# Two MLPs behind an attention: where the raw words of the up weights land, and when two pairs of weights are decoded

## The chip, the cores and the metric

The kernel runs on one core of a Trainium2 chip. The metric is the device time of one execution in microseconds; the kernel before took 832.86, 834.61 and 835.45 us in three runs, median 834.61. Its engines are TensorE (PE: matrix products), VectorE (DVE) and ScalarE (ACT: elementwise work), GpSimd (POOL) and SyncE (SP, which issues DMAs). The engines work from queues of their own and wait for each other by semaphores.

## The reference

An attention over 4 batches of 544 rows in 8 heads of 64 (32 global rows that see everything, 512 local rows that see a band and the global ones), and behind it two MLPs of 2304 rows:

```
x = attention(q, k, v)                     # 2304 x 512
h = x @ w_in ;  g = where(h > 0, h, exp(min(h, 0)) - 1) ;  x = g @ w_out
h = x @ w_in2;  g = 0 below -1, h above 1, (h + 1)**2 / 4 between;  out = g @ w_out2
```

w_in is 512 x 2048, w_out 2048 x 512. The weights come as 64-bit numbers.

## The kernel before

The attention takes the first 127 us or so; then come the MLPs. PE works in a 32-bit format with a shortened mantissa, so every operand is split into a high and a low part and every product is three (low x high, high x low, high x high). The 64-bit weights are split on the chip by `decode` (L200): the two halves of each number are unpacked by seven steps on DVE (L217 to L240) and two on ACT (L214 and the copy of the high part, L238). Step L239, `power`, isolates the exponent and writes it over the raw words, which are no longer needed then; L240 makes the low part of it.

The hidden width of 2048 goes in blocks of 128 (`f`), mostly in pairs of blocks: pairs n = 0 to 5 belong to layer 0, 6 to 13 to layer 1. The four token batches of 512 go in two duos. For a pair and a duo, a 2 x 2 block product is made by seven products instead of eight (`quad`, four parts; each product is 6 matmuls, L1064). For it the weights of a pair are wanted as they are and in four mixtures (S1 to S4), and the tokens in seven forms (X11 to T4). `decode_in(n)` makes the weights: `words` (L868) loads the raw words, two DMAs of 512 KB into one of the two buffers `wraw` that all raw words and sums share; then `decode`, `whole` (high + low), four additions `mixed`, and their split (ACT L912, DVE L862). The result is `wi`, one tile per pair with the weights in its first half and the mixtures in the second, in one of three places (n mod 3). `decode_out(n)` does the same for the down weights (`wo`).

DVE also joins the products (`u`, L862), makes the nonlinearity (with ACT; `g`, `gl`), and adds down products to sums. Each product needs one of four PSUM banks in rotation, so PE's next product in a bank waits for DVE (or ACT, L1094) to have read the last one.

Between the layers the tokens' forms are made anew: `later_forms(duo)` takes the sums of layer 0 (`so_far`, loaded again from DRAM by L1163 and L1166), mixes them on DVE, splits each form (`split`: ACT L954, DVE L862) and stores it to DRAM (`keep`, L961). The forms of batches 2 and 3, `later_forms(1)`, come in the second half of chunk 2, those of batches 0 and 1 in chunk 3.

What sets the order: the program runs through 7 chunks of 17 events, one chunk per two pairs and some 87 us each. In an event one part of a `quad` is issued; `job_at` puts jobs (decodes, forms) on a line at an event of a chunk, and a job does a step per event. From the program so written a scheduler makes each engine's fixed order. All DMAs from SP go out in one order.

```
job_at(at + 1, decode_out(2 * c + 1))
job_at(at + 5, decode_in(2 * c + 2));  job_at(at + 8, decode_out(2 * c + 2))
c == 2: job_at(at + 9, later_forms(1), False)     else: job_at(at + 12, decode_in(2 * c + 3))
c == 3: job_at(at, decode_in(7)); job_at(at + 2, decode_out(7)); job_at(at + 4, later_forms(0), False)
```

Of the kernel before, what the change touches and what calls it, by code (L numbers as in the profile page):

```python
# [9 lines left out]
F32 = mybir.dt.float32  # L10
# [68 lines left out]
def band_attention_then_two_mlps(  # L79
# [120 lines left out]
    def decode(wtmp_p, raw, hi, lo):  # L200

        n = raw.shape[1]
        words = raw.bitcast(U32).rearrange("p (n two) -> p n two", two=2)
        low, high = words[:, :, 0], words[:, :, 1]
        top = wtmp_p.tile([P, n], U32, tag="top", name="top")
        if eng is pinned:
            power = wtmp_p.tile([P, n], U32, tag="power", name="power")
        else:
            power = raw.bitcast(U32)[:, 0:n]
        rest = wtmp_p.tile([P, n], U32, tag="rest", name="rest")  # L210
# [646 lines left out]

    pairs_in, slot = {}, {}

# [24 lines left out]
    def of_pair(n):  # L884

        layer, q = (0, n + 2) if n < 6 else (1, n - 6)
        return layer, (2 * q, 2 * q + 1)

    def decode_in(n):

        layer, fs = of_pair(n)
        raw = words(KT * P, [(w1, w2)[layer][f][:, 0:KT * P] for f in fs])
        yield
# [3 lines left out]
        for _ in decode(wtmp_p, raw, w[:, 0, 0:4 * BLOCK], w[:, 1, 0:4 * BLOCK]):  # L897
            pass
        yield
# [3 lines left out]
        whole = add(  # L903
            x, w[:, 0, 0:4 * BLOCK].bitcast(F32), w[:, 1, 0:4 * BLOCK].bitcast(F32)
        )
# [5 lines left out]
        hi = w[:, 0, 4 * BLOCK:]  # L911
        eng.scalar.activation(hi, y, AF.Copy)  # L912
        add(w[:, 1, 4 * BLOCK:], y, hi.bitcast(F32), ALU.subtract)
        pairs_in[n] = w
        rows_in[1, n] = lambda k, part: w[:, part, 0:4 * BLOCK].rearrange("p (f c) -> p f c", f=2)[
            :, :, k * P:(k + 1) * P
        ]
# [48 lines left out]
    def first_forms(duo):  # L966
# [20 lines left out]
        for i, pair in enumerate((((T2, x22), (T3, x12)), ((T1, x11), (T4, x21)))):  # L987
            if duo == 0:

                t = w_ps[0].tile([P, 2, 2, 2 * SL], F32R, tag=f"wi{i}", name="form")  # L990
            for k, (form, src) in enumerate(pair):
                out = new_form(form) if duo else [t[:, k, part] for part in range(2)]
# [7 lines left out]
    def later_forms(duo):  # L1000

# [43 lines left out]
    born = {(0, f, j): -LAG for f, j in [(f, j) for j in range(B) for f in EARLY][:UP_EARLY]}  # L1045
    made_forms, holds, summed, w_out_uses = set(), {}, {}, {}

# [10 lines left out]
    def product(n, duo, col, i, then):  # L1058

        need(lambda: n in pairs_in and holds.get(i) == (of_pair(n)[0], duo))  # L1060
        ps, w, x = up_bank(), pairs_in[n], slot[i]
        for k in range(2):
            for t, (a, b) in enumerate(((1, 0), (0, 1), (0, 0))):
                eng.tensor.matmul(  # L1064
                    ps,
                    w[:, a, col + k * P:col + (k + 1) * P],
                    x[b][:, k * SL:(k + 1) * SL],
# [77 lines left out]
    def pop():  # L1145
# [7 lines left out]
        else:  # L1153
# [3 lines left out]
            if f == fs[2 % len(fs)] and NF - 1 in fs:  # L1157

                if layer == 0 and j < 2:
                    if j == 0:  # L1160
                        spare.append(w_ps[1].tile([P, 2, 2 * BLOCK * 4], F32, tag="wi2", name="sums"))
                    so_far[layer, j] = spare[0][:, j % 2].rearrange("p (k n) -> p k n", k=KT)
                    eng.sync.dma_start(so_far[layer, j], sums[layer + 1, j])  # L1163
# [9 lines left out]

    spare = []
    pair_of = {(of_pair(n)[0], f): n for n in range(14) for f in of_pair(n)[1]}
# [81 lines left out]
    for c in range(7):  # L1257
        at = base + 17 * c
        if c == 3:

            job_at(at, decode_in(7))
            job_at(at + 2, decode_out(7))
            job_at(at + 4, later_forms(0), False)
# [4 lines left out]
        job_at(at + 1, decode_out(2 * c + 1))  # L1268
        if c < 6:
            job_at(at + 5, decode_in(2 * c + 2))  # L1270
            job_at(at + 8, decode_out(2 * c + 2))
            if c == 2:
                job_at(at + 9, later_forms(1), False)
            else:
                job_at(at + 12, decode_in(2 * c + 3))
    for g, (c, duo) in enumerate(groups):
# [90 lines left out]
```

## Time and profile before

| | before |
|---|---|
| median of 3 runs, us | 834.61 (832.86 to 835.45) |
| profiled execution, us | 831.0 |
| span of its trace, us | 829.2 |
| PE busy | 805.8 us, 97% |
| DVE busy | 683.4 us, 82% |
| ACT busy | 547.2 us, 66% |
| granted PE clock | 1.00 |
| DMA | 172.49 MB, mean 208 GB/s |

Start with the busy shares in equal windows of 20 us: a share over the whole span hides where an engine is full and where it isn't. Then look, in the window where PE is not full, at what ended each of its idle times (the timeline of PE), and go on to the engine named there. Times count from the span's start.

### The profile page before, as it was taken

The numbers are of one execution on the slowest core, as the hardware profiler recorded it, in microseconds if no ns is written. First come the engines' busy times: TensorE is split into PE (matmuls) and PEld (weight loads), VectorE is DVE, ScalarE is ACT, GpSimd is POOL, SyncE is SP. The second block draws the span as 40 slices with busy tenths as digits, with TensorE's granted clock in tenths as the row PEclk, the third lists the DMA queues.
The fourth block names the chain that finished last, engine by engine and source line by source line (L and its number), as shares of the span: only waits on it lengthen the run. The fifth ranks groups of instructions, "written<-read, shape, count | busy, mean of one in ns | idle before, by whom it ended". The sixth has DMA issues, their size and how long they took to land.

```text
span 829.2 us, 15816 instructions
## 1 busy us (share of the span) xinstructions
PE 805.8 (97%) x6058; PEld 659.1 (79%) x6058; DVE 683.4 (82%) x1276; ACT 547.2 (66%) x929; POOL 87.7 (11%) x146
## 2 busy tenths in 40 slices
PE   7899899999999999999999979999999999999998
PEld 5677778888888888888888856888888888888886
DVE  5898979997989789867879899999988797845563
ACT  5888865675576656656555658778867786766451
POOL 2232200000011111111000000000110202011000
PEclk9999999999999999999999999999999999999999
DMA  8988828787966498629727667539671995369533
GB/s 284 330 272 273 253 89 295 263 343 256 357 169 143 99 278 265 120 22 292 245 90 290 228 247 261 153 122 303 202 161 25 263 296 107 46 172 291 198 106 110
DMA packets 63676, 172.49 MB, mean 208 GB/s; under 512 B 8944, under 2 KB 9200, under 8 KB 62448
## 3 DMA queue, kind: packets, MB, share of 16 engines
q1 hardware_dynamic: 54096, 154.43, 53.7%
q0 software_dynamic: 9216, 16.78, 13.1%
q8 instruction: 48, 0.79, 0.4%
q10 hardware_dynamic: 288, 0.26, 0.1%
q14 instruction: 28, 0.23, 0.1%
HBM read 112.46 MB, written 58.98 MB: 207 GB/s over the span
## 4 chain that ended last, share of the span: by engine, by line
PE 82%; DVE 6%; DMA 5%; ACT 4%; issue 2%; SPq 0%; DVEq 0%; ACTq 0%
PE dn L369 38%; PE up L1064 29%; PE up L282 4%; PE up L294 2%; DMA wraw<-in_w 2%; PE dn L382 2%; DMA v_sb<-in_vwin 2%; ACT sn L147 1%; PE s L147 1%; PE up L147 1%; DVE u L862 1%; PE pt L147 1%; DVE xl L862 1%; ACT pT L147 1%; PE po L147 1%
## 5 line engine op out<-in xcount | busy, mean ns | idle before, releaser
L1064 PE MATMUL up<-xh,wi 128*128 128x512 f32 x784 | 259.9, 391 | 5.0 <-DVE u L862 2.5
L369 PE MATMUL dn<-gh,wo 128*128 128x512 f32 x608 | 181.4, 390 | 0.0
L1064 PEld LDWEIGHTS up<-xh,wi 128*128 128x128 f32 x784 | 147.2, 188 | 37.2 <-DVE u L862 3.6
L862 DVE TENSOR_TENSOR u<-up,u 128x512 f32<-128x512 f32 x196 | 131.8, 688 | 48.7 <-PE up L1064 47.6
L1064 PE MATMUL up<-xl,wi 128*128 128x512 f32 x392 | 152.8, 390 | 0.0
L369 PEld LDWEIGHTS dn<-gh,wo 128*128 128x128 f32 x608 | 114.0, 188 | 23.6
L353 POOL DMA_DIRECT2D sum<-ev x64 | 58.6, 1211 | 589.7 <-ACT ev L348 588.8
L331 ACT ACTIVATE gh<-g 128x512 fp32r<-128x512 f32 x123 | 77.0, 628 | 56.5 <-DVE g L314 27.8
L369 PE MATMUL dn<-gl,wo 128*128 128x512 f32 x304 | 111.8, 390 | 0.5 <-DVE gl L335 0.5
L335 DVE TENSOR_TENSOR gl<-g,gh 128x512 fp32r<-128x512 f32 x123 | 84.4, 689 | 17.3 <-ACT gh L331 17.2
L1064 PEld LDWEIGHTS up<-xl,wi 128*128 128x128 f32 x392 | 73.7, 188 | 14.7
L307 ACT ACTIVATE g<-u,half_sb 128x512 f32<-128x512 f32 x64 | 46.1, 721 | 42.8 <-DVE u L862 37.7
L369 PEld LDWEIGHTS dn<-gl,wo 128*128 128x128 f32 x304 | 57.0, 188 | 12.7 <-DVE gl L335 1.0
L369 PE MATMUL dn<-gh,xl 128*128 128x512 f32 x160 | 62.7, 393 | 0.5 <-DVE sum L356 0.4
L348 ACT ACTIVATE ev<-dn 128x512 f32<-128x512 f32 x96 | 53.5, 598 | 14.6 <-PE dn L369 13.5
L369 PE MATMUL dn<-gh,xh 128*128 128x512 f32 x160 | 62.4, 390 | 0.0
L316 DVE TENSOR_TENSOR g<-u,g 128x512 f32<-128x512 f32 x64 | 43.9, 688 | 20.9 <-ACT g L309 20.8
L369 PE MATMUL dn<-gl,xh 128*128 128x512 f32 x160 | 59.0, 390 | 0.0
L302 ACT ACTIVATE g<-u 128x512 f32<-128x512 f32 x48 | 30.2, 630 | 35.8 <-DVE u L862 29.4
L308 ACT ACTIVATE g<-g,one_sb 128x512 f32<-128x512 f32 x68 | 49.1, 721 | 1.4
L304 ACT ACTIVATE g<-g,one_sb 128x512 f32<-128x512 f32 x63 | 45.5, 722 | 1.5
L309 ACT ACTIVATE g<-g 128x512 f32<-128x512 f32 x68 | 42.8, 629 | 1.2
(190 smaller groups left out, 1354.1 us busy)
## 6 DMA issues: line engine op xcount, KB each, us to landing
wraw<-in_w SPq DMA_DIRECT2D x56, 512.0 KB, 6.6
xl<-form SPq DMA_DIRECT2D x42, 512.0 KB, 6.9
xh<-form SPq DMA_DIRECT2D x42, 512.0 KB, 8.7
v_sb<-in_vwin SPq DMA_DIRECT2D x64, 260.0 KB, 4.7
sum<-ev POOLq DMA_DIRECT2D x64, 256.0 KB, 8.0
form<-xh SPq DMA_DIRECT2D x24, 512.0 KB, 3.6
form<-xl SPq DMA_DIRECT2D x24, 512.0 KB, 4.7
sum<-ev SPq DMA_DIRECT2D x32, 256.0 KB, 4.7
```

The costliest lines, as they stand in the source:

```text
L147: return lambda *args, **kw: tc.keep_in_program_order(fn(*args, **kw))
L304: eng.scalar.activation(self.g, self.g, AF.Relu, bias=one_sb, scale=-1.0)
L307: eng.scalar.activation(self.g, self.ps, AF.Relu, bias=half_sb, scale=-0.5)
L308: eng.scalar.activation(self.g, self.g, AF.Relu, bias=one_sb, scale=-1.0)
L316: eng.vector.tensor_tensor(g, self.ps, g, ALU.max)
L331: eng.scalar.activation(self.gh, self.g, AF.Copy)
L335: eng.vector.tensor_tensor(self.gl, self.g, self.gh.bitcast(F32), ALU.subtract)
L348: eng.scalar.activation(out, ps, AF.Copy)
L353: eng.gpsimd.dma_start(to, out, accum_op=ALU.add)
L369: eng.tensor.matmul(banks[d], w[:, d * P:(d + 1) * P], g, start=first and k == 0, stop=last and k == 2)
L862: return eng.vector.tensor_tensor(out, a, b, op)
L1064: eng.tensor.matmul(ps, w[:, a, col + k * P:col + (k + 1) * P], x[b][:, k * SL:(k + 1) * SL], start=k + t == 0, stop=k == 1 and t == 2,)
```

## The change

Three things are changed.

1. The pair's tile `wi` is cut in two: `wi` for the weights and `ws` for the mixtures. The raw words land in `ws` (`words_in`, L893), since the mixtures are only made when the words have been used up. The load is issued right behind the last of the 14 products of pair n - 3, which held the place; it waits for that product. Pair 8 is the exception: its place holds the sums between, so `decode_in` loads it itself. The buffers `wraw` keep the down weights and some sums.
2. Since the low half of `ws` is not free during the decode, `power` is written over `top` and no longer over the raw words. With it, step L237 (L239 before) waits for ACT's copy out of `top`.
3. Pair 6 is decoded from event 2 of chunk 2 on (5 before), its down weights from event 4 (8 before). Pair 7 (`seventh`) is decoded inside `later_forms(1)`, between the first subtractions and `mixed`; before, that was at chunk 3's start. Its down weights come one event earlier.

The number of instructions on each engine is the same.

```diff
 def decode(wtmp_p, raw, hi, lo):
-        if eng is pinned: power = wtmp_p.tile([P, n], U32, tag="power", name="power")
-        else: power = raw.bitcast(U32)[:, 0:n]
+        power = wtmp_p.tile([P, n], U32, tag="power", name="power") if eng is pinned else top
...
+    def words_in(n):
+        layer, fs = of_pair(n)
+        raw_in[n] = w_ps[n % 3 // 2].tile([P, 4 * BLOCK], U64, tag=f"ws{n % 3}", name="wraw")
+        for i, f in enumerate(fs):
+            eng.sync.dma_start(
+                raw_in[n][:, i * KT * P:(i + 1) * KT * P], (w1, w2)[layer][f][:, 0:KT * P]
+            )
 def decode_in(n):
-        raw = words(KT * P, [(w1, w2)[layer][f][:, 0:KT * P] for f in fs])
-        while n == 2 and len(w_ps) < 2:
+        while n == 2 and len(w_ps) < 2 or w_in_uses.get(n - 3):
             yield
-        w = w_ps[n % 3 // 2].tile([P, 2, 8 * BLOCK], F32R, tag=f"wi{n % 3}", name="wi")
+        if n not in raw_in:
+            words_in(n)
+            yield
+        w = pool.tile([P, 2, 4 * BLOCK], F32R, tag=f"wi{k}", name="wi")
...
+        ws = pool.tile([P, 2, 4 * BLOCK], F32R, tag=f"ws{k}", name="ws")
+        eng.scalar.activation(ws[:, 0], y, AF.Copy)
+        add(ws[:, 1], y, ws[:, 0].bitcast(F32), ALU.subtract)
+        pairs_in[n] = w, ws
 def later_forms(duo, between=None):
...
         add(x12, x22, x12, ALU.subtract)
+        while between is not None and 7 not in decoded:
+            next(between)
+            yield
         mixed = wtmp_p.tile([P, 2 * SL], F32, tag="top", name="mixed")
 def product(n, duo, col, i, then):
+        w_in_uses[n] -= 1
+        if not w_in_uses[n] and n + 3 < 14 and n != 5:
+            words_in(n + 3)
 # the table of jobs
         if c == 3:
-            job_at(at, decode_in(7))
-            job_at(at + 2, decode_out(7))
+            job_at(at, seventh)
+            job_at(at + 1, decode_out(7))
...
+        if c == 2:
+            job_at(at + 2, decode_in(6))
+            job_at(at + 4, decode_out(6))
+            seventh = decode_in(7)
+            job_at(at + 9, later_forms(1, seventh), False)
```

The first place is the SP queue at the end of layer 0. `wraw<-in_w x2` are the two DMAs of raw words of pair 7 (the first such row of each piece), `form_1_k` the stores of the new forms of batches 2 and 3, `sums<-sum_0` and `sums<-sum_1` the loads of the sums of batches 0 and 1. Before:

```order
L1163 DMA sums<-sum_0_107 128x2048
L961 DMA form_1_3_139<-xl 128x1024
L961 DMA form_1_6_142<-xh 128x1024
L961 DMA form_1_2_138<-xl 128x1024
L1163 DMA sums<-sum_1_108 128x2048
L961 DMA form_1_5_141<-xl 128x1024
L868 DMA wraw<-in_w 128x512 x2
L961 DMA form_1_6_142<-xl 128x1024
L868 DMA wraw<-in_w 128x512 x4
```

And with the change:

```order
L1183 DMA sum<-sum_3_110 128x2048
L893 DMA wraw<-in_w 128x512 x2
L973 DMA form_1_0_136<-xh 128x1024
L973 DMA form_1_1_137<-xh 128x1024
L973 DMA form_1_0_136<-xl 128x1024
L973 DMA form_1_1_137<-xl 128x1024
L973 DMA form_1_3_139<-xh 128x1024
L1180 DMA sums<-sum_0_107 128x2048
```

The words of pair 7 stood behind nearly all stores of the forms and both loads of the sums, and now stand ahead of all of them, next after the load of batch 3's sums.

The second place is DVE, where the `rest` step of pair 7's decode stands. Before, the stretch in which batch 3's sums are finished and the first products of pair 6 arrive (`u_5830<-up_5823` is its first join) ran on without it:

```order
L356 TENSOR_TENSOR sum_5768<-dn_5679,sum_5768 128x512
L314 SCALAR_TENSOR_TENSOR g_5790<-u_5648,g_5790 128x512
L862 TENSOR_TENSOR u_5830<-up_5823,u_5821 128x512
L862 TENSOR_TENSOR xl_5855<-sum_5570,xh_5854 128x1024
L335 TENSOR_TENSOR gl_5796<-g_5790,gh_5794 128x512
L862 TENSOR_TENSOR u_5821<-up_5860,u_5821 128x512
L862 TENSOR_TENSOR xl_5901<-sum_5570,xh_5900 128x1024
```

and the step came much later, behind the first sums of the next layer's batch (the decode has the number 6060):

```order
L356 TENSOR_TENSOR sums_5985<-dn_6080,sums_5985 128x512
L217 TENSOR_SCALAR rest_6098<-wraw_6060 128x1024
L335 TENSOR_TENSOR gl_6125<-g_6118,gh_6123 128x512
L229 TENSOR_SCALAR top_6097<-top_6097 128x1024
L221 SCALAR_TENSOR_TENSOR rest_6098<-wraw_6060,rest_6098 128x1024
L233 TENSOR_SCALAR top_6097<-top_6097 128x1024
```

With the change it stands ahead of that first join (here `u_5842<-up_5835`; the decode has the number 5792):

```order
L354 TENSOR_TENSOR sum_5777<-dn_5697,sum_5777 128x512
L312 SCALAR_TENSOR_TENSOR g_5802<-u_5670,g_5802 128x512
L354 TENSOR_TENSOR sum_5777<-dn_5701,sum_5777 128x512
L215 TENSOR_SCALAR rest_5968<-wraw_5792 128x1024
L333 TENSOR_TENSOR gl_5808<-g_5802,gh_5806 128x512
L219 SCALAR_TENSOR_TENSOR rest_5968<-wraw_5792,rest_5968 128x1024
L860 TENSOR_TENSOR u_5842<-up_5835,u_5833 128x512
L860 TENSOR_TENSOR xl_5867<-sum_5604,xh_5866 128x1024
L227 TENSOR_SCALAR top_5967<-top_5967 128x1024
L860 TENSOR_TENSOR u_5833<-up_5872,u_5833 128x512
```

Pair 7's decode has moved ahead of the joins of chunk 3's first products, and among the new forms (`xl<-sum,xh`).

The third place is DVE some 70 us later: the join of the product A12 x X21 of pair 6 for the other duo, with the work that stands around it. Before (`u_6480<-up_6473`):

```order
L217 TENSOR_SCALAR rest_6550<-wraw_6516 128x1024
L316 TENSOR_TENSOR g_6325<-u_6274,g_6325 128x512
L862 TENSOR_TENSOR u_6480<-up_6473,u_6471 128x512
L862 TENSOR_TENSOR sums_5985<-sums_5985,mixed_6348 128x1024
L862 TENSOR_TENSOR xl_6352<-mixed_6348,xh_6351 128x1024
L221 SCALAR_TENSOR_TENSOR rest_6550<-wraw_6516,rest_6550 128x1024
```

and with the change (`u_6491<-up_6484`):

```order
L860 TENSOR_TENSOR sums_5994<-sums_5994,mixed_6359 128x1024
L314 TENSOR_TENSOR g_6319<-u_6316,g_6319 128x512
L860 TENSOR_TENSOR xl_6363<-mixed_6359,xh_6362 128x1024
L860 TENSOR_TENSOR u_6491<-up_6484,u_6482 128x512
L314 TENSOR_TENSOR g_6336<-u_6285,g_6336 128x512
L860 TENSOR_TENSOR xl_6410<-sums_5994,xh_6409 128x1024
L333 TENSOR_TENSOR gl_6326<-g_6319,gh_6324 128x512
L333 TENSOR_TENSOR gl_6343<-g_6336,gh_6341 128x512
L215 TENSOR_SCALAR rest_6561<-wraw_6527 128x1024
```

Before, the first step of the decode of pair 8 (`rest_6550`) stood ahead of this join; now it stands five rows behind, and the sum of the forms and the low part of T2 have moved ahead of it.

## Rows read from the trace of the kernel before

**Rows 1.** Windows by stage: PE, PEld, DVE, ACT, POOL busy (instructions), clock, DMA share, GB/s.

```profile
460.00:480.00 20.00, 19.86 (x88) 16.10 (x88) 18.21 (x27) 10.03 (x15) 0.00 (x0) 1.00 0.49 179
480.00:500.00 20.00, 14.20 (x69) 10.73 (x67) 19.91 (x26) 13.61 (x17) 0.00 (x0) 1.00 0.75 290
500.00:520.00 20.00, 19.00 (x80) 14.81 (x81) 19.83 (x27) 17.14 (x27) 0.00 (x0) 1.00 0.73 256
```

**Rows 2.** Timeline of PE, 479 to 511: start, us, operation, idle before and releaser.

```profile
479.08 0.39 PE L1064 MATMUL up<-xh,wi 128*128 128x512 f32 x1
...
482.95 0.50 PE L1064 MATMUL up<-xh,wi 128*128 128x512 f32 x1 [0.98 <-DVE u L862]
...
486.35 0.50 PE L1064 MATMUL up<-xh,wi 128*128 128x512 f32 x1 [1.74 <-DVE wi L862]
...
493.37 0.39 PE L294 MATMUL up<-wi,xh 128*128 128x256 f32 x1 [1.22 <-DVE u L862]
...
497.97 0.50 PE L1064 MATMUL up<-xh,wi 128*128 128x512 f32 x1 [1.48 <-DVE u L862]
...
500.32 0.50 PE L1064 MATMUL up<-xh,wi 128*128 128x512 f32 x1 [0.69 <-ACT u L1094]
...
506.18 0.50 PE L1064 MATMUL up<-xh,wi 128*128 128x512 f32 x1
...
510.19 1.20 PE L369 MATMUL dn<-gl,wo 128*128 128x512 f32 x4 [0.53 <-DVE gl L335]
```

**Rows 3.** Timeline of DVE, 432 to 508.

```profile
432.19 0.69 DVE L862 TENSOR_TENSOR u<-up,u 128x512 f32<-128x512 f32 x1 [1.50 <-PE up L1064]
...
467.85 0.69 DVE L217 TENSOR_SCALAR rest<-wraw 128x1024 uint32<-128x1024 uint32 x1 [1.67 <-DMA wraw<-in_w]
...
505.43 0.70 DVE L862 TENSOR_TENSOR u<-up,u 128x512 f32<-128x512 f32 x1
506.03 1.23 DVE L862 TENSOR_TENSOR sums<-sums,mixed 128x1024 f32<-128x1024 f32 x1
507.17 1.23 DVE L862 TENSOR_TENSOR xl<-mixed,xh 128x1024 fp32r<-128x1024 f32 x1
```

**Rows 4.** Timeline of the SP queue (SPq), 417 to 452: DMA issues.

```profile
417.31 0.32 SPq L1166 DMA_DIRECT2D sum<-sum  x1
432.33 1.79 SPq L961 DMA_DIRECT2D form<-xh  x2
...
451.79 1.25 SPq L868 DMA_DIRECT2D wraw<-in_w  x2
```

**Rows 5.** The chain that ended last: start, us, link.

```profile
452.55 15.21 DMA wraw<-in_w
```

**Rows 6.** DMA issues from 451.5, 478 and 599: KB each, us to landing.

```profile
wraw<-in_w SPq DMA_DIRECT2D x2, 512.0 KB, 14.4
...
wraw<-in_w SPq DMA_DIRECT2D x2, 512.0 KB, 4.9
...
wraw<-in_w SPq DMA_DIRECT2D x2, 512.0 KB, 8.2
```

**Rows 7.** Timeline of PE: last matmul of pair 4.

```profile
426.25 0.39 PE L1064 MATMUL up<-xh,wi 128*128 128x512 f32 x1
```

**Rows 8.** Windows by stage, columns as in rows 1.

```profile
425.00:433.00 8.00, 8.00 (x37) 6.64 (x36) 6.34 (x11) 4.47 (x8) 0.00 (x0) 1.00 0.00 0
247.00:262.00 15.00, 15.00 (x68) 12.42 (x67) 14.97 (x22) 9.81 (x16) 3.95 (x4) 1.00 0.93 185
```

**Rows 9.** Groups by line and form: busy us, mean ns, idle before.

```profile
L233 DVE TENSOR_SCALAR top<-top 128x1024 uint32<-128x1024 uint32 x29 | 20.0, 691 | 0.1
...
L239 DVE TENSOR_SCALAR wraw<-top 128x1024 uint32<-128x1024 uint32 x29 | 20.0, 690 | 0.0
...
L862 DVE TENSOR_TENSOR mixed<-whole 128x256 f32<-128x256 f32 x28 | 10.6, 422 | 0.1
...
L238 ACT ACTIVATE wi<-top 128x1024 fp32r<-128x1024 f32 x14 | 14.8, 1057 | 3.1 <-DVE top L234 3.0
```

More of the change, by code (lines that the diff above doesn't have):

```diff
@@ L200, in decode @@
     def decode(wtmp_p, raw, hi, lo):
-        n = raw.shape[1]
-        words = raw.bitcast(U32).rearrange("p (n two) -> p n two", two=2)
+        raw = raw.bitcast(U32)
+        n = raw.shape[1] // 2
+        words = raw.rearrange("p (n two) -> p n two", two=2)
         low, high = words[:, :, 0], words[:, :, 1]
         top = wtmp_p.tile([P, n], U32, tag="top", name="top")
[L206 to L209, printed above, removed]
+        power = wtmp_p.tile([P, n], U32, tag="power", name="power") if eng is pinned else top
         rest = wtmp_p.tile([P, n], U32, tag="rest", name="rest")
@@ L856, in band_attention_then_two_mlps @@
     ps_dn.append(mpool("ps_dn1", 1, space=PSUM))
-    pairs_in, slot = {}, {}
+    pairs_in, slot, raw_in, decoded = {}, {}, {}, set()
     def add(out, a, b, op=ALU.add):
@@ L887, in of_pair @@
         return layer, (2 * q, 2 * q + 1)
+    def words_in(n):
[5 more added lines that the diff above has]
+            )
     def decode_in(n):
         layer, fs = of_pair(n)
-        raw = words(KT * P, [(w1, w2)[layer][f][:, 0:KT * P] for f in fs])
-        yield
-        while n == 2 and len(w_ps) < 2:
+        while n == 2 and len(w_ps) < 2 or w_in_uses.get(n - 3):
             yield
-        w = w_ps[n % 3 // 2].tile([P, 2, 8 * BLOCK], F32R, tag=f"wi{n % 3}", name="wi")
-        for _ in decode(wtmp_p, raw, w[:, 0, 0:4 * BLOCK], w[:, 1, 0:4 * BLOCK]):
+        pool, k = w_ps[n % 3 // 2], n % 3
+        if n not in raw_in:
+            words_in(n)
+            yield
+        raw = raw_in[n]
+        w = pool.tile([P, 2, 4 * BLOCK], F32R, tag=f"wi{k}", name="wi")
+        for _ in decode(wtmp_p, raw, w[:, 0], w[:, 1]):
             pass
+        decoded.add(n)
         yield
@@ L910, in decode_in @@
         add(at(y, S4), at(x, A12), at(y, S2), ALU.subtract)
[L911 to L915, printed above, removed]
+        ws = pool.tile([P, 2, 4 * BLOCK], F32R, tag=f"ws{k}", name="ws")
+        eng.scalar.activation(ws[:, 0], y, AF.Copy)
+        add(ws[:, 1], y, ws[:, 0].bitcast(F32), ALU.subtract)
+        pairs_in[n] = w, ws
+        rows_in[1, n] = lambda k, part: w[:, part].rearrange("p (f c) -> p f c", f=2)[
             :, :, k * P:(k + 1) * P
@@ L988, in first_forms @@
             if duo == 0:
-                t = w_ps[0].tile([P, 2, 2, 2 * SL], F32R, tag=f"wi{i}", name="form")
+                t = [w_ps[0].tile([P, 2, 2 * SL], F32R, tag=f"w{c}{i}", name="form") for c in "is"]
             for k, (form, src) in enumerate(pair):
-                out = new_form(form) if duo else [t[:, k, part] for part in range(2)]
+                out = new_form(form) if duo else [t[k][:, part] for part in range(2)]
                 last_split[0] = split(out, src)
@@ L998, in first_forms, with later_forms @@
                 yield
-    def later_forms(duo):
+    def later_forms(duo, between=None):
         j0, j1 = 2 * duo, 2 * duo + 1
@@ L1159, in pop @@
                 if layer == 0 and j < 2:
-                    if j == 0:
-                        spare.append(w_ps[1].tile([P, 2, 2 * BLOCK * 4], F32, tag="wi2", name="sums"))
-                    so_far[layer, j] = spare[0][:, j % 2].rearrange("p (k n) -> p k n", k=KT)
+                    so_far[layer, j] = w_ps[1].tile([P, KT, SL], F32, tag=("wi2", "ws2")[j], name="sums")
                     eng.sync.dma_start(so_far[layer, j], sums[layer + 1, j])
@@ L1172, in pop @@
                 w_out_uses[pair_of[layer, f]] -= 1
-    spare = []
+    w_in_uses.update({n: 14 for n in range(14)})
     pair_of = {(of_pair(n)[0], f): n for n in range(14) for f in of_pair(n)[1]}
```

16 lines of the change are left out of this document (7 added, 9 removed).

## The prediction

> **What bounds the kernel now.** I read the windows by stage first. TensorE (PE) is full in every 20 us window between 120 and 460 us and again from 520 to 800 (8.00 of 8 and 15.00 of 15 us in two pieces of it), at a granted clock of 1.00 (the 2.4 GHz level) [rows 8], so in those stretches nothing that VectorE (DVE), ScalarE (ACT) or the DMA queues do can gain anything; it can only lose. The one hole in the middle of the program is the passage from layer 0 to layer 1 [rows 1]: from 460 to 520 PE is busy 19.86, 14.20 and 19.00 of 20 us, while DVE is at 19.9. The ends of the program (attention before 120, the tail after 820) keep their order in this change, so the whole question is those 40 us and whether a new hole opens elsewhere.
>
> Next, the PE timeline of that passage [rows 2]. The reader is to see that nearly every idle time there ends on a DVE operation: 0.98, 1.74, 1.22, 1.48 and 0.53 us behind `u`, `wi`, `u`, `u` and `gl`, and one of 0.69 behind an ACT copy that itself came late. The listed gaps (6.6 us) are less than the loss, because PE also restarts slowly after each. The loss itself: the matmuls from 479.08 to the product that restarts at 506.18 make 19.2 us of work at the pace of the full windows (a 512-wide one every 0.227 us, as 479.08 and the rows behind it run), but they took 27.1: 7.9 us lost there. By the same count up to 520 it is 9.3. **So 9.3 us is the most that mending this passage can give.**
>
> Then the DVE timeline [rows 3]: at 467.85 DVE starts the `rest` step of pair 7's decode, after 1.67 us in which it waited for that pair's raw words by DMA. From there to 520 it never rests, and PE lives on what it delivers. The chain that ended last says the same: the transfer of those words, 15.21 us, is a link of it [rows 5]. The SP queue [rows 4] says why it is late: SP had nothing to issue between 417.31 and the form stores that begin at 432.3, but pair 7's words go out only at 451.79, among those stores and the loads of the sums, and so land in 14.4 us on average, where two transfers of the same size alone on the DMA engines took 4.9 [rows 6].
>
> **The change, part by part.**
>
> *Place of the raw words.* Pair 7's two DMAs (L893) now stand on SP ahead of all form stores and wait only for pair 4's last product. In PE's present order the last matmul of that product starts at 426.25 and runs 0.39 [rows 7]; with the release I take 427.1 for the issue. The DMA engines carry nothing from 425 to 433 [rows 8]. The quiet pair of DMAs [rows 6] was 0.4 apart at issue and its second landed 5.8 us after the first went out; I take that, so the words are there at 433.0. DVE, whose order is now another, reaches the `rest` step where it used to sit idle before 432.19 (1.50 us, waiting for PE) [rows 3]: at about 430.7. DVE takes its instructions in order, as the waiting `rest` at 467.85 showed, so this one now holds up everything behind it for 2.4 us, to 433.1.
>
> The Trainium skill, Perfetto Trace Analysis, on the Tensor Engine Instruction, says so of DVE generally (its queue is strictly first in, first out); the row at 467.85 agrees.
>
> *What DVE must then do.* Between that `rest` and the copy `u_6491<-up_6484` stand 51 operations of 512 wide, 29 two-source ones of 1024 wide, 8 single-source ones of 1024 wide and 4 of 256 wide. From one start to the next these take 0.60 (505.43 to 506.03), 1.14 (506.03 to 507.17) [rows 3], 0.60 (busy 0.69 [rows 9], less the same overlap) and 0.38 (0.42 [rows 9]). That is 30.6 + 33.1 + 4.8 + 1.5 = 70.0 us, so the copy starts at 503.1 and ends 0.69 later, at 503.8. The same count on the kernel before, from 467.85 to the copy at 505.43, gives 37.2 against 37.6 measured, so I add 0.4 to 0.7 for small stalls: 504.3. PE's next product in that bank has the same 19.2 us of work ahead of it after 479.08 as the one that restarted at 506.18, so it would be due at 498.3. It is **6.0 us late, against 7.9**. Behind this point before lost another 1.4; now the next DVE steps (two `gl`, one `sum` of forms) have their due times moved by those 6 us, and I take 0.5. **Loss 6.5 instead of 9.3: a gain of 2.8 us.**
>
> Both ends: if the words were there when DVE comes (430.7), the copy ends 2.4 earlier, the loss is about 4.1 and the gain 5.2. If they land 4 us later than taken (437), the gain is gone. If they take the 14.4 us of the loaded rows [rows 6], DVE starts at 442, the loss is about 15 and the kernel is 6 slower. I take 5.8 since rows 8 show the engines empty at that time.
>
> The Trainium skill, DMA: Bandwidth & Descriptors, in the section on the anatomy of one DMA (of the GpSimd path), gives a fixed 2.0 us plus bytes at 436 GB/s; an estimate for both DMAs by that page is 4.4 us, which would put the gain near 4.2. The row with 5.8 decides here.
>
> *In-place power.* L237 writes over `top` and not over the raw words: `L233` is such a step in place and takes 691 ns, `L239` 690 [rows 9]; no cost in itself. But it now waits for ACT's copy of the high part (1.06 [rows 9]). In most of the 29 decodes two to six DVE operations stand between, 1.2 us or more; where it is bare the wait is at most 0.3 us, hidden everywhere that PE is full. I take nothing; bound 0 to 1 us at the passage.
>
> *Moved decodes of pairs 6 and 7 and the waits of `so_far`.* No instruction is added: the counts on every engine stay. Their DVE work, 13 us a decode, goes from behind 467 to before it; that is the count above. The second raw load of pair 7 (the down weights) lands by 463 to 470 when its slot frees at about 457, DVE comes at about 471.5 (38 us of work behind 433.1): in time, but closely. A miss costs as much as it is late.
>
> *The other pairs.* Words of pairs 0, 1, 2, 3, 5, 9, 11 and 13 are now issued only when a place is free, where they used to have two buffers of their own. Counting DVE's work back from the product that needs it, as above, words may land at latest at (release, latest landing): pair 3 254.9, 266; pair 5 339.7, 350; pair 9 517.7, 531; pair 11 603.6, 613.7; pair 13 691.1, 701. With 6 to 8 us each (8.2 in the window at 600 [rows 6]) all make it, pairs 3 and 11 by 2 us. Taken as nothing; bound 0 to 6 us in all.
>
> The Trainium skill speaks against this part: DMA: Bandwidth & Descriptors, Rules for kernel authors, wants a DMA issued early and waited for late. That rule is the second rival.
>
> The sum: the profiled execution takes 831.0 (span 829.2), 3.6 under the median of 834.61. It would take 828.2; on the median, **831.8 us**.
>
> **The rivals.** A difference under 0.3% (2.5 us) can hardly be told from none.
>
> *The wait only moves* (chance 0.37 within 0.3%). DVE has as much to do as before, and its idle time ahead of the passage is what can be won: the two largest pieces are 1.50 and 1.67 us [rows 3], and 2.4 are given back at 430.7. For it: DVE stays the bound from 433 to 504 in my own count. If 1 to 3 us more of small stalls (ACT copies, form stores that a new form must wait for) come in those 70 us of dense work, the gain is 0 to 2: 833.5 us.
>
> *Words too late, slower* (0.15). In a stretch where PE is full, a `rest` at the head of DVE's queue waits for words that could go out only when the place was free. Places: pair 3 at 255 to 266, where the DMA engines are 0.93 busy [rows 8], and pair 11. It decides when a landing takes over 10 to 11 us: at the 14.4 of the loaded rows [rows 6] it is 3 to 4 us late, and in a stretch where PE has no slack of its own all of it is lost. Two such pairs at 3.5 each against the gain of 2.8 make 838.8 us; one of them alone ends near 835.3, within 0.3%. Against it: pair 3's window is loaded by 256 KB accumulations that are half gone by 262, and PE's banks let DVE be a little late.
>
> *More is won* (part of faster, 0.12). The words land in under 4.5 us, or DVE reaches `rest` later than 430.7, and the loss falls to 4 to 5: 829.5 us.
>
> *The forecast*, gain of 2 to 4: 0.36. Together: faster by over 0.3% 0.47 (the forecast's better part and the greater gain), same 0.38, slower 0.15. The likeliest time of 831.8 lies just past the bound. The range goes from 828.3 (gain of 5.2 and 1 of the median's spread of 832.86 to 835.45) to 836.6 (no gain and one pair late by 2); the double miss at 838.8 is left out.
>
> **What would show it.** Right: the DMA of pair 7 issued at about 427 and landed before 434; a DVE wait on it of 2 to 3 us near 431 and none at 467; PE windows 480 to 520 with 36 us busy where 33.2 were; first PE gaps behind DVE `xl` or `u` from about 459 on, 6 us in all by 504. Wrong: PE under 20.00 in a window outside 455 to 515 with DVE `rest` or ACT `top` waiting for `wraw`; the issue later than 430; or a PE loss in the passage of over 9.

## The result, and the profile after

The change makes the kernel **slower by 0.63%**: 839.55 us (median of 20 runs, 834.75 to 843.73) against 833.82 (20 runs, 831.22 to 836.06), ratio 1.0063, 95% interval 1.0046 to 1.0079. Forecast were 831.8 and a range up to 836.6. The profiled execution took 835.08 us (span 833.3), 4.1 more than the one before; in both kernels the profiled execution lies below the median.

The windows by stage (columns as in [rows 1]), of the change:

```profile
460.00:480.00 20.00, 18.73 (x82) 15.02 (x81) 19.90 (x31) 12.70 (x19) 0.00 (x0) 1.00 0.62 220
480.00:500.00 20.00, 19.31 (x97) 16.12 (x95) 20.00 (x27) 12.59 (x17) 0.00 (x0) 1.00 0.79 281
500.00:520.00 20.00, 13.23 (x50) 10.20 (x49) 15.93 (x21) 14.19 (x23) 0.00 (x0) 0.83 0.67 219
```

Where before lost most of its time between 480 and 500 [rows 1], the change loses 2.7 us from 440 to 500 and then 6.8 in one window, in which the granted clock is also 0.83. In this execution PE is at 19.99 or 20.00 of 20 in every window between 120 and 440 and between 520 and 800. The timeline of PE in the passage:

```profile
455.87 0.50 PE L1083 MATMUL up<-xh,ws 128*128 128x512 f32 x1 [0.69 <-ACT u L1113]
...
461.80 0.50 PE L1083 MATMUL up<-xh,wi 128*128 128x512 f32 x1 [1.27 <-ACT xh L966]
...
498.73 0.50 PE L1083 MATMUL up<-xh,ws 128*128 128x512 f32 x1 [0.69 <-ACT u L1113]
...
503.57 0.50 PE L1083 MATMUL up<-xh,ws 128*128 128x512 f32 x1 [0.92 <-DVE u L860]
...
513.79 0.80 PE L367 MATMUL dn<-gh,xl 128*128 128x512 f32 x1 [5.85 <-ACT ev L346]
514.38 0.63 PE L367 MATMUL dn<-gh,xh 128*128 128x512 f32 x1
```

The five idle times behind `u`, `wi` and `gl` [rows 2] have become three of 0.7 to 1.3 us behind ACT, one of 0.92 behind the join, and one of 5.85 us that before does not have, behind `ev`, ACT's copy of a down product out of PSUM. The rows from 514.38 on follow at 0.43 us from one to the next; from 517.67 on it is 0.23 again. The timeline of DVE, at the three places of the prediction:

```profile
432.96 0.69 DVE L215 TENSOR_SCALAR rest<-wraw 128x1024 uint32<-128x1024 uint32 x1 [1.49 <-DMA wraw<-in_w]
...
502.83 0.68 DVE L860 TENSOR_TENSOR u<-up,u 128x512 f32<-128x512 f32 x1
...
508.67 0.69 DVE L215 TENSOR_SCALAR rest<-wraw 128x1024 uint32<-128x1024 uint32 x1 [2.22 <-DMA wraw<-in_w]
```

The wait for pair 7's words is at 432.96 instead of 467.85 [rows 3], and the join of A12 x X21 starts at 502.83 (503.1 was forecast). Then DVE waits 2.22 us for words again, those of **pair 8**. The SP queue:

```profile
427.18 0.81 SPq L893 DMA_DIRECT2D wraw<-in_w  x2
...
500.18 0.32 SPq L973 DMA_DIRECT2D form<-xh  x1
500.55 1.25 SPq L893 DMA_DIRECT2D wraw<-in_w  x2
```

Pair 7's words go out at 427.18 (427.1 forecast). Those of pair 8 go out at 500.55. Before, they went out 22 us earlier, into the shared buffer that pair 7's up words had left, and landed by 484.6:

```profile
478.79 0.80 SPq L868 DMA_DIRECT2D wraw<-in_w  x2
```

Now their place is `ws2`, which holds the sums of batch 1 until the last new form made from them is split, at 498.2 (the last DVE operation on it starts at 497.02). The other 2.3 us up to 500.55 are the order on SP: ahead of the two loads stands a store of a form, which waits for ACT's copy of that form and goes out at 500.18. The chain that ended last goes through this transfer, straight to the down product that waited:

```profile
501.02 7.55 DMA wraw<-in_w
513.79 8.36 PE dn L367 x28
```

What lies between the two is ACT's timeline:

```profile
508.66 1.15 ACT L212 ACTIVATE top<-wraw 128x1024 f32<-128x1024 f32 x1 [3.88 <-DMA wraw<-in_w]
509.70 0.72 ACT L305 ACTIVATE g<-u,half_sb 128x512 f32<-128x512 f32 x1
510.31 0.69 ACT L305 ACTIVATE g<-up,half_sb 128x512 f32<-128x512 f32 x1
510.88 1.33 ACT L306 ACTIVATE g<-g,one_sb 128x512 f32<-128x512 f32 x2
512.11 1.15 ACT L307 ACTIVATE g<-g 128x512 f32<-128x512 f32 x2
513.14 2.06 ACT L346 ACTIVATE ev<-dn 128x512 f32<-128x512 f32 x4
```

The first ACT step of pair 8's decode, L212, reads the raw words and waits 3.88 us for them. ACT does nothing else meanwhile, and behind it stand, in its fixed order, two curves `g` and only then the four `ev` copies (the last row, 2.06 us) that free the four down banks PE needs. The transfer itself took 7.55 us; that is neither quick nor slow beside [rows 6].

The Trainium skill, Perfetto Trace Analysis, on the Tensor Engine Instruction, says that ACT, like DVE, takes its queue strictly in order; the rows above agree: the `ev` copies, whose products PE had finished before 508, ran at 513.14, behind a step that had no data.

Last, the clock, in windows of 2 us (columns as in [rows 1]):

```profile
507.00:509.00 2.00, 0.94 (x5) 0.44 (x3) 0.33 (x1) 0.34 (x1) 0.00 (x0) 1.00 1.02 408
509.00:511.00 2.00, 0.00 (x0) 0.00 (x0) 1.52 (x3) 2.00 (x4) 0.00 (x0) 0.92 0.93 371
511.00:513.00 2.00, 0.00 (x0) 0.00 (x0) 1.51 (x3) 2.00 (x4) 0.00 (x0) 0.50 0.16 64
513.00:515.00 2.00, 1.21 (x3) 1.02 (x4) 2.00 (x3) 2.00 (x5) 0.00 (x0) 0.50 0.21 77
515.00:517.00 2.00, 2.00 (x7) 1.54 (x6) 1.19 (x3) 2.00 (x4) 0.00 (x0) 0.50 1.07 355
517.00:519.00 2.00, 2.00 (x9) 1.66 (x8) 1.93 (x3) 1.63 (x3) 0.00 (x0) 0.88 0.29 98
```

PE did its last matmul before 508. From 510.7 the granted clock is 0.50 (the 1.2 GHz level), and it stays there until 517.5, while PE has been at work again since 513.79. The nine matmuls from there to 517.67 took 3.9 us where 2.0 would do at the usual pace: 1.8 us lost.

**How the loss of the passage is measured below.** ACT's copy of the first product of a pair starts, where ACT waited for PE, 0.5 us behind PE; its time less the matmul work that PE had to do until then (0.227 us a 512-wide matmul) is PE's lateness at that point. The growth of this lateness from the copy near 410 us to the one near 595 us is the loss of the passage, whatever the attention at the beginning took: 10.1 us before, 13.8 with the change. Along PE's rows, 5.5 of the 13.8 are lost until the product that restarts at 503.57 (before lost 8.6 until the same product, at 506.18), and 8.1 behind it, where before lost 1.4: 6.0 in the wait for `ev`, 1.8 by the clock, 0.3 in restarts. The remaining 0.2 is the precision of this count. (The prediction counts from 479.08, where before was 0.7 late already; on its count the 5.5 and 8.6 are 4.8 and 7.9.) So **the passage did become better by 3 us, up to 503, and gave back 7 in the 15 us behind it.**

### The profile page after: what moved, and what is told of

Same layout as the page of the kernel before. It is cut to its first block, busy times and chain, and to the rows that moved or that the text cites. A ratio compares the mean times of both kernels' runs of the same rounds, so it can differ in the third digit from the quotient of the medians.

```text
span 833.3 us, 15795 instructions
## 1 busy us (share of the span) xinstructions
PE 808.0 (97%) x6058; PEld 661.1 (79%) x6058; DVE 684.4 (82%) x1276; ACT 543.8 (65%) x929; POOL 87.4 (10%) x146
## 4 chain that ended last, share of the span: by engine, by line
PE 82%; DVE 7%; ACT 5%; DMA 4%; issue 2%; SPq 0%; POOL 0%; DVEq 0%; ACTq 0%; POOLq 0%
PE dn L367 38%; PE up L1083 29%; PE up L280 4%; PE up L292 2%; PE dn L380 2%; DMA wraw<-in_w 2%; ACT sn L147 1%; PE s L147 1%; DMA k_sb<-in_kT 1%; PE up L147 1%; ACT pT L147 1%; PE pt L147 1%; DVE u L860 1%; DVE xl L860 1%; ACT g L147 1%
## 5 line engine op out<-in xcount | busy, mean ns | idle before, releaser
L1083 PE MATMUL up<-xh,ws 128*128 128x512 f32 x448 | 153.2, 392 | 2.3 <-ACT u L1113 1.4
L1083 PE MATMUL up<-xh,wi 128*128 128x512 f32 x336 | 114.2, 390 | 1.3 <-ACT xh L966 1.3
L1083 PEld LDWEIGHTS up<-xh,ws 128*128 128x128 f32 x448 | 84.1, 188 | 20.8 <-ACT u L1113 2.2
L1083 PE MATMUL up<-xl,ws 128*128 128x512 f32 x224 | 87.3, 390 | 0.0
L1083 PEld LDWEIGHTS up<-xh,wi 128*128 128x128 f32 x336 | 63.1, 188 | 15.2 <-ACT xh L966 1.7
L1083 PE MATMUL up<-xl,wi 128*128 128x512 f32 x168 | 65.4, 389 | 0.0
L346 ACT ACTIVATE ev<-dn 128x512 f32<-128x512 f32 x96 | 53.7, 598 | 13.4 <-PE dn L367 11.3
L306 ACT ACTIVATE g<-g,one_sb 128x512 f32<-128x512 f32 x68 | 48.7, 721 | 1.4
```

Of the source, the lines that this page charges most:

```text
L306: eng.scalar.activation(self.g, self.g, AF.Relu, bias=one_sb, scale=-1.0)
L346: eng.scalar.activation(out, ps, AF.Copy)
L1083: eng.tensor.matmul(ps, w[:, a, at + k * P:at + (k + 1) * P], x[b][:, k * SL:(k + 1) * SL], start=k + t == 0, stop=k == 1 and t == 2,)
```

## The experiments

Each ratio is to runs of the kernel before that were taken along with that kernel (their medians lie between 833.4 and 834.2); the loss is that of one profiled execution.

| kernel | ratio to before (interval) | median, us | loss of the passage, us |
|---|---|---|---|
| before | 1 | 833.82 | 10.1 |
| change | 1.0063 (1.0046 to 1.0079) | 839.55 | 13.8 |
| e1 words of pair 8 in a shared buffer | 1.0031 (1.0015 to 1.0048) | 836.40 | 11.3 |
| e2 ACT's step behind the ev copies | 1.0003 (0.9986 to 1.0021) | 834.06 | 9.9 |
| e3 before, with pair 6 early | 1.0079 (1.0055 to 1.0103) | 840.43 | 16.3 |
| e4 places alone | 1.0018 (1.0001 to 1.0036) | 835.65 | 11.3 |
| e5 the change again | 1.0070 (1.0047 to 1.0093) | 839.73 | 14.0 |
| e6 e1 and e2, and DVE's step behind the join | 0.9963 (0.9947 to 0.9979) | 831.43 | 8.0 |
| e10 e6 without the moved decodes | 0.9975 (0.9958 to 0.9993) | 831.22 | 6.2 |
| e11 e6 again | 0.9982 (0.9966 to 0.9997) | 832.41 | 8.0 |
| e8 the gap filled with matmuls | 1.0052 (1.0035 to 1.0068) | 837.81 | 12.1 |

**e1: the words of pair 8 early.** The theory: those words, late, are the cost.

```diff
 def decode_in(n):
+        if n == 8:
+            raw_in[n] = words(KT * P, [(w1, w2)[layer][f][:, 0:KT * P] for f in fs])
+            yield
         if n not in raw_in:
             words_in(n)
```

> The change, but the raw words of pair 8 land in one of the two shared buffers, as before, and not in the place that the sums still hold; the orders of PE, ACT and DVE stay as in the change up to pair 8's decode. Theory (the loss behind 503 us is those words: ACT's first step on them stands ahead of the four ev copies for which PE waits, and the long idle time then costs clock): the words land before 485, the idle time of 5.85 us and the window at clock 0.83 go, and the profiled span falls from 833.3 by about 7 us (5.85 and some 2 of clock, less 1 for what is late next) to 825 to 828; ratio to the kernel before 0.991 to 0.997. Rival 1 (the moved decodes themselves overload DVE, the words only arrive when they can be used): a gap of 3 to 6 us stays near 507, ratio 1.002 to 1.008. Rival 2 (the buffer taken away makes the down words of pair 8 or 9 late): the gap moves behind 515 and ends on wo, ratio 0.998 to 1.004.

The 5.85 us behind `ev` are gone, but the passage still loses 11.3 us. PE's timeline of e1:

```profile
506.35 0.66 PE L1086 MATMUL up<-xh,ws 128*128 128x512 f32 x1 [2.65 <-DVE u L860]
...
514.18 0.66 PE L320 MATMUL up<-eye_sb,g 128*128 128x128 f32 x4 [1.87 <-DVE g L314]
```

And DVE's, around the join (505.62 is `u_6491<-up_6484`):

```profile
498.07 0.68 DVE L215 TENSOR_SCALAR rest<-wraw 128x1024 uint32<-128x1024 uint32 x1
...
503.34 1.21 DVE L219 SCALAR_TENSOR_TENSOR rest<-wraw,rest 128x1024 uint32<-128x1024 uint32 x1
...
505.62 0.68 DVE L860 TENSOR_TENSOR u<-up,u 128x512 f32<-128x512 f32 x1
```

The scheduler knew that the words were there and put the first two DVE steps of the decode (0.60 and 1.14 us) ahead of the join. The join is late by these, PE waits 2.65 us for it instead of 0.92, and its clock is at 0.50 for 3.4 us behind that. So the edit was no clean test: it took the late words away and added a new delay. Rival 2 falls, since the idle times end on `u` and `g` and not on `wo`. Rival 1's ratio came out and its gap nearly did (2.65 us where it gave 3 to 6), but not its reason: the moved decodes of pairs 6 and 7 are in the change too, where the same gap is 0.92; what is new ahead of the join are pair 8's two steps.

**e2: the order on ACT alone.** The words land as late as in the change; only L212 is put behind the four `ev` (`after` is the newest `ev` copy, for pair 8 alone).

```diff
             ins = eng.scalar.activation(top.bitcast(F32), high.bitcast(F32), AF.Abs)
             in_order("top", ins)
+            if after is not None:
+                tc.add_manual_dep(ins.ins, after.ins.name, IN_ORDER, reason="behind ev")
```

> The change, but ACT's first step on pair 8's words (the absolute value, L212) is put behind the four ev copies that stood six rows behind it; the words land where and when they did, at about 508.5, and DVE's rest step still waits for them. Theory (what stops PE is the order in ACT's queue, not the late words as such): the ev copies run at 506 to 508, PE's idle time there falls from 5.85 to under 1.5 us, no stretch at a lower clock, span 826 to 829, ratio 0.993 to 0.999. Rival 1 (DVE's wait of 2.2 us for the same words, or what comes after the decode, is what PE would wait for anyway): a gap of 3 us or more stays, ending on DVE u, g or gl, ratio 1.001 to 1.006.

PE's wait for `ev` in e2:

```profile
515.55 0.67 PE L372 MATMUL dn<-gh,xl 128*128 128x512 f32 x1 [2.04 <-ACT ev L351]
```

And ACT, which now waits for DVE's `gl` ahead of the two curves and for no words:

```profile
511.45 0.73 ACT L310 ACTIVATE g<-u,half_sb 128x512 f32<-128x512 f32 x1 [1.11 <-DVE gl L338]
```

The wait for `ev` falls from 5.85 to 2.04 us and the loss of the passage from 13.8 to 9.9; the kernel is as fast as before. The remaining 2 us and a low stretch of 3.4 us behind them are more than the theory allowed. They too come from ACT's order: the six steps of the two curves, from 511.45 on, still stand ahead of the `ev` copies, which begin at 514.91. So the place of L212 in ACT's queue made 3.9 us of the loss, about as much as the change had lost against before (3.7). The late words as such did not make them: DVE's step still waits for them here, 2.98 us.

**e3: pair 6 early, in the kernel before.**

```diff
-            job_at(at + 5, decode_in(2 * c + 2))
-            job_at(at + 8, decode_out(2 * c + 2))
+            job_at(at + (2 if c == 2 else 5), decode_in(2 * c + 2))
+            job_at(at + (4 if c == 2 else 8), decode_out(2 * c + 2))
```

> The kernel before with only pair 6's decode moved (event 2 of chunk 2 for 5, its down weights at 4 for 8); raw words in the shared buffers, pair 7 at chunk 3's beginning as before. Theory: the passage is set by what DVE must do behind pair 7's words, so this alone leaves the loss near 9 us: ratio 0.998 to 1.002. Rival (pair 6's decode is what crowds DVE ahead of the passage): DVE reaches the forms earlier and the passage loses 6 to 7 us: ratio 0.995 to 0.998.

Neither: 6 us worse than before. The DVE step on pair 7's words:

```profile
470.86 0.69 DVE L217 TENSOR_SCALAR rest<-wraw 128x1024 uint32<-128x1024 uint32 x1 [2.21 <-DMA wraw<-in_w]
```

DVE has time to spare before 470 and waits 2.21 us for pair 7's words, whose transfer took 15.1 us as in the kernel before; then PE waits 3.5 and 3.3 us on DVE, with two stretches at half clock (3.4 and 6.8 us). So an earlier decode of pair 6 did not help: DVE waited for the words of pair 7 all the same. It loses 6 us more than before; counted along PE's rows, 4.4 of them lie in the two stretches at half clock, which before does not have. Why PE's idle time comes in longer pieces here was not taken apart.

**e4: the places without the moved decodes.** The change with the table of jobs of before:

```diff
-            job_at(at, seventh)
-            job_at(at + 1, decode_out(7))
+            job_at(at, decode_in(7))
+            job_at(at + 2, decode_out(7))
...
-            job_at(at + 2, decode_in(6))
-            job_at(at + 4, decode_out(6))
-            seventh = decode_in(7)
-            job_at(at + 9, later_forms(1, seventh), False)
+            job_at(at + 5, decode_in(6))
+            job_at(at + 8, decode_out(6))
+            job_at(at + 9, later_forms(1), False)
```

> The change with the old table of jobs: raw words land in the pair's own place, power over top, but pairs 6 and 7 decoded as in the kernel before. Theory: pair 7's decode stands late on DVE again, so PE loses some 7 to 10 us in the passage up to 510, and pair 8's words still wait for the sums' place, so that a gap of 2 to 6 us with a lower clock comes behind it: ratio 1.003 to 1.012, slower than or equal to the full change. Rival (the moved decodes do the harm and the places none): ratio 0.998 to 1.002.

PE and ACT of e4 behind 502:

```profile
502.98 0.39 PE L1083 MATMUL up<-xh,ws 128*128 128x512 f32 x1
...
511.61 0.74 PE L367 MATMUL dn<-gh,xl 128*128 128x512 f32 x1 [4.39 <-ACT ev L346]
```

```profile
509.34 1.16 ACT L212 ACTIVATE top<-wraw 128x1024 f32<-128x1024 f32 x1 [3.70 <-DMA wraw<-in_w]
510.41 0.66 ACT L305 ACTIVATE g<-up,half_sb 128x512 f32<-128x512 f32 x1
510.98 2.04 ACT L346 ACTIVATE ev<-dn 128x512 f32<-128x512 f32 x4
```

The ratio of 1.0018 is under what the theory gave, and its first half fell: the product of S1 x T1 starts at 502.98, no later than in the change (503.57), without the moved decodes. The new places, with which pair 7's words go out at 427.36, were enough for what was won up to there: DVE takes the `rest` step of pair 7 at 433.11, as in the change, although its decode was not moved in the table of jobs. The second half held: PE waits 4.39 us for `ev` behind the same late words (their DMA goes out at 501.2). The words come no earlier than in the change, but only one step of 0.66 us stands between L212 and the `ev` copies here, six steps of 3.4 us there; so the change's idle time is 1.5 us longer. Its low stretch is 6.8 us against 3.4. By the ratio alone the rival (0.998 to 1.002) fits as well, and it is half right: the places alone lose 11.3 us in the passage, 1.2 more than before, and the moved decodes add another 2.5. They do so early: the change has lost 3.4 us by 464, e4 0.3 by 480.

**e5 and e9: the change again.** The profile of the change lay below its median, so it was taken three more times.

> The change itself, once more, beside the runs below on the same chip. Its first profile (835.08 us) lay 4.5 us under its median (839.55), and its runs spread over 9 us where those of before spread over 5. Theory: the idle time of 5.85 us behind 507 is there in every run, and what differs is how long PE works at half clock behind it (6.83 us in the first profile): ratio 1.004 to 1.008, an idle time of 5 to 7 us ending on ev, a low stretch behind it of 3 us or more. Rival (the spread comes from elsewhere, as the attention at the beginning): the passage loses the same 13.7 us as in the first profile and the rest is lost before 120 us.

> The change, a third profile, to see what lies between its profiles so far (passage loss 13.7 and 14.0 us) and its median, which is 2 to 4 us above them. Theory: in the slower runs PE's low clock comes in more or longer stretches, at the passage: loss there 15 us or more if the run is over 839 us. Rival: the passage loses the same 13.5 to 14.2 us in every run, and the rest comes and goes in the attention at the beginning (where the offset of PE's first 78 us of product work has been 126.5 and 127.9 us so far, and 126.2 to 131.0 in all profiles, the kernel before among them).

> As the third look: over 839 us with a passage loss of 15 us or more by the theory, with 13.5 to 14.2 and an offset of 129 us or more from the attention by the rival.

These executions took 837.0, 840.18 and 837.98 us. The idle time behind `ev` was 6.55, 5.79 and 5.71 us, the low stretch behind it 6.8, 3.4 and 6.8, and the passage lost 14.0, 13.1 and 14.2 us. The one of them that took over 839 us lost no more in the passage than the others, against the theory. The two ACT copies between which the loss is taken, in the change's first profile:

```profile
409.47 0.60 ACT L1113 ACTIVATE u<-up 128x512 f32<-128x512 f32 x1 [0.82 <-PE up L1083]
...
596.74 0.60 ACT L1113 ACTIVATE u<-up 128x512 f32<-128x512 f32 x1 [0.48 <-PE up L1083]
```

From copy to copy these are 187.27 us; in the execution of 840.18 us, with the same work, 186.62 (from 415.00 to 601.62). That execution is 5.5 us later already at the first copy. Most of this comes from the attention: at a copy near 230 us it is 4.3 us later, and the lateness at that copy varied from 126.2 to 131.0 us over the profiles of all kernels, the kernel before and e3 (whose attention is that of before) at 126.2 and 129.8. Stretches of 3.4 us at half clock lie in the attention in two of these executions (one at 27.0 us in that of 840.18, two at 53.5 and 121.8 in that of 837.98), but e8, the latest of all, has none there, so they are not the whole reason.

The other 1.2 us are pair 3's words, outside the passage. DVE and PE in the execution of 840.18 us:

```profile
270.42 0.69 DVE L215 TENSOR_SCALAR rest<-wraw 128x1024 uint32<-128x1024 uint32 x1 [6.16 <-DMA wraw<-in_w]
...
271.63 0.68 DVE L386 TENSOR_TENSOR rows_sum<-dn,rows_sum 128x512 f32<-128x512 f32 x1
...
272.37 0.50 PE L367 MATMUL dn<-gh,xl 128*128 128x512 f32 x1 [1.11 <-DVE rows_sum L386]
```

DVE waits 6.16 us for these words, and the step for which PE waits stands two places behind. In the change's first profile DVE's wait was 4.97 us and PE had no such gap; in the other two it was 5.24 and 5.19 with gaps of 0.20 and 0.14, in e2 6.29 with 1.30. The kernel before and e3 have neither the wait nor the gap. That the change's median lies 5.7 us above that of before, and its loss in the passage only 3.7, is within the interval of the ratio (3.8 to 6.6 us) almost; pair 3's words explain up to about 1 us of the rest, and what remains stays open.

**e8: the gap filled.** Does the idle time cost clock on top of itself? One product of pair 6 is computed four times into its own bank, behind the last down product and ahead of the group that waits. The output is the same, PE has 18 matmuls more.

```diff
+        for again in range(4 if (n, duo, col) == (6, 0, S1) else 1):
             ...
+                    if again:
+                        tc.add_manual_dep(ins.ins, last_dn[0].ins.name, IN_ORDER, reason="behind dn")
```

> The change, with one product of pair 6 (S1 x T1 of batches 0 and 1) computed four times into its bank where once would do: the 18 added matmuls (4.1 us at full clock) stand on PE exactly where it waited for the ev copies, between the last down product of the group and the next group. The output is the same. Theory (idle PE time there costs clock, on top of the 5.85 us themselves): the idle time shrinks to about 1.8 us, no or a shorter low stretch behind it, so that with MORE work the kernel gets 1 to 4 us faster than the change: span of 830 to 832.5, ratio to before 1.000 to 1.004, spread of the runs smaller. Rival (the clock falls whatever PE does there, or costs nothing by itself): time as the change, or up to 4 us more, ratio 1.006 to 1.011.

PE's timeline (the added matmuls run from 513.34 to 517.4) and the window with its clock:

```profile
513.34 0.39 PE L1088 MATMUL up<-xh,ws 128*128 128x512 f32 x1
...
519.43 0.50 PE L369 MATMUL dn<-gh,xl 128*128 128x512 f32 x1 [1.85 <-ACT ev L346]
```

```profile
500.00:520.00 20.00, 16.54 (x72) 12.77 (x71) 16.72 (x21) 13.29 (x21) 0.00 (x0) 1.00 0.72 252
```

The idle time is 1.85 us, the clock stays at 1.00, and the passage loses 12.1 us, 4.1 of them work that was added: 1.7 to 1.9 us less than the change. The median is 1.9 under that of e5, taken beside it. So idle PE time cost clock here, and in the passage 4.1 us of useless matmuls were cheaper than none. The ratio of 1.0052 is above the range given and, with six runs each, its interval overlaps that of e5; the trace carries this reading, and the medians agree with it in direction and size.

**e6: all three put right.** Words of pair 8 in a shared buffer, L212 behind the `ev` copies, and DVE's `rest` step behind the join (`behind` is that join, for pair 8 alone):

```diff
         in_order("rest", ins)
+        if behind is not None:
+            tc.add_manual_dep(ins.ins, behind.ins.name, IN_ORDER, reason="behind the join")
```

> The change with pair 8's words in a shared buffer (as in e1), ACT's first step on them behind the four ev copies (as in e2), and DVE's rest step behind the join of A12 x X21 of pair 6, where the change had it and e1 did not. Theory (late words, ACT's order and DVE's two early steps were the three costs): the join ends near 503, PE's idle time behind it is under 1.5 us, no low clock in the passage, which loses 6 to 8 us against 10.1 of before and 13.7 of the change; ratio 0.995 to 0.998, faster than both kernels. Rival 1 (DVE is full in any case, so that the next join or gl is late instead): a loss of 9 to 11 us and ratio 0.999 to 1.003. Rival 2 (down words of pair 8 or 9 are late): an idle time behind 515 on wo or ws, ratio over 1.001.

PE's timeline of e6, and the window with its clock:

```profile
507.51 0.50 PE L1091 MATMUL up<-xh,ws 128*128 128x512 f32 x1 [0.91 <-DVE u L865]
...
509.37 2.11 PE L372 MATMUL dn<-gh,wo 128*128 128x512 f32 x8 [0.21 <-ACT gh L334]
512.18 1.20 PE L372 MATMUL dn<-gl,wo 128*128 128x512 f32 x4 [0.71 <-DVE gl L338]
513.68 0.50 PE L372 MATMUL dn<-gh,xl 128*128 128x512 f32 x1 [0.30 <-ACT ev L351]
```

```profile
500.00:520.00 20.00, 17.17 (x71) 12.64 (x70) 16.20 (x21) 15.68 (x25) 0.00 (x0) 1.00 0.58 220
```

The passage loses 8.0 us, no low clock in it, and the idle times behind the join's 0.91 are 0.21, 0.71 and 0.30. Ratio 0.9963, as the theory had it: **faster than both kernels**, by 2.0 us than before. It shows what early words for pair 7 are good for once pair 8's decode does not stand in the way: 10.1 to 8.0.

**e10 and e11: e6 without the moved decodes.** The table of jobs of e4 in e6, and e6 again on the same chip.

> e6 with the table of jobs of the kernel before, that is, without the moved decodes of pairs 6 and 7: places, power over top, pair 8's words in a shared buffer, and its first steps behind ev and behind the join. What is open: whether the moved decodes have a part in what e6 won. Theory after e4 (early words of pair 7 were enough): as good as e6, the passage loses 7 to 9 us, ratio 0.994 to 0.998. Rival (DVE's work of pair 7's decode, 13 us, falls into the passage again): DVE is late behind 480, the passage loses 9.5 to 12 us, ratio 0.999 to 1.003.

> e6 once more, beside e10 on the same chip: ratio 0.994 to 0.998, loss of the passage 7.5 to 8.5 us, no stretch at a lower clock in it.

PE's timeline of e10:

```profile
497.31 0.50 PE L1091 MATMUL up<-xh,wi 128*128 128x512 f32 x1 [1.47 <-DVE u L865]
...
508.39 1.19 PE L372 MATMUL dn<-gl,wo 128*128 128x512 f32 x4 [0.79 <-DVE gl L338]
```

The passage loses 6.2 us, the least of all kernels, against 8.0 in both profiles of e6. So the moved decodes have no part in what was won, and in the passage they cost 1.8 us. In the medians the two lie 1.2 us apart, with intervals that overlap; both are faster than before.

## Why the prediction was wrong

*Right.* The hole in the passage and its size; the issue of pair 7's words at 427.1 (427.18); DVE's wait for them, 2.4 forecast and 1.49 measured; the 70 us of DVE work to the join, 503.1 against 502.83; PE late there by 6.0 forecast and 4.8 measured. But the gain up to there is owed to the new places, with which the words go out early, and not to the decodes that were moved: these cost 1.8 to 2.5 us in the passage (e10 against e6, e4 against the change). Power in place cost nothing that PE saw, although DVE waits for ACT in it 7.8 us in all (before none) and up to 2.0 at once, where at most 0.3 was forecast. For raw words DVE now waits 18.3 us instead of 6.3:

```profile
L215 DVE TENSOR_SCALAR rest<-wraw 128x1024 uint32<-128x1024 uint32 x29 | 20.0, 691 | 18.6 <-DMA wraw<-in_w 18.3
...
L237 DVE TENSOR_SCALAR top<-top 128x1024 uint32<-128x1024 uint32 x29 | 20.0, 689 | 7.8 <-ACT xh L236 3.6 <-ACT wo L236 3.3 <-ACT wi L236 0.8
```

In the first profile PE stayed full wherever these waits fell outside the passage. In other executions it did not: pair 3's words cost PE 1.11 us near 270 in the execution of 840.18 us and 1.30 in e2. So the prediction's sign of being wrong, PE under 20.00 in a window outside 455 to 515 with `rest` waiting for `wraw`, came true (18.89 of 20 from 260 to 280 in the execution of 840.18 us), and so did another, a loss of over 9 us in the passage.

*The step that failed* is "Behind this point before lost another 1.4; now the next DVE steps ... have their due times moved by those 6 us, and I take 0.5". It measured 8.1 us. Three things were missing from it. First, the list of pairs whose words now come late named 0, 1, 2, 3, 5, 9, 11 and 13, and not pair 8, the one exception in the change: its words may only go out when the sums have left `ws2`, at 498.2, and with SP's order went out at 500.55, where before they went out at 478.79. Second, that step counted DVE alone. ACT reads the raw words too, its step stands ahead of the `ev` copies, and PE needs the banks that these free; e2 shows that this order makes 3.9 of the 13.8 us. Third, a single long idle time lowered PE's clock, which cost another 1.8 us (e8 got 1.7 to 1.9 back); before, with about the same idle time in pieces of at most 1.74 us, the clock had not fallen in the profiled execution.

*The rivals.* "Words too late, slower", given 0.15, is the one that came true in kind: words that could go out only when the place was free, and an engine that takes its queue in order. It was priced for pairs 3 and 11 and for DVE. At 838.8 us it came nearest the measured time, but by luck: pair 11 cost PE nothing in these traces, pair 3 up to 1.3 us, and neither is what made the loss. The rule of the Trainium skill beside it (DMA: Bandwidth & Descriptors, Rules for kernel authors: issue early, wait late) agrees with the traces: the issue at 500.55 instead of 478.79 is what made pair 8 late. The range ended at 836.6 because this rival was cut off there.

## What to carry to other kernels

When a buffer is given up, list every transfer that used it with the time at which its new place comes free, the exceptions in the code first; the one that breaks the rule of the others is the one to work out. For each late transfer look at every engine that reads it, and at what stands behind that reader in its queue: here the harm was done by a reader nobody was in a hurry for. And what is won ahead of a wait for a landing can be lost again in it: here 3 us were won up to 503, and the wait behind it took 6.

## What the runs showed of the hardware that was not expected

In the idle time that ended on `ev` the granted clock went to 0.50 and stayed there for 6.8 us in three of four executions of the change, through 2.8 to 5.2 us in which PE was at work again, and for 3.4 us in the fourth. The length did not follow the idle time: 5.71 us of it came with 6.8, 5.79 with 3.4. With idle times of 2.0 to 4.4 us (e1, e2, e4) it was 3.4 us at that level, with 3.48 and 3.32 (e3) 3.4 and 6.8; in e8 and e6, with idle times up to 1.85 us, it did not fall in the passage.
